# One kernel, one core: the last weight tiles of the final layer split earlier, and some subtractions placed elsewhere

## The chip, the core and the metric

The kernel runs on one core of a Trainium2 chip. TensorE (PE in the rows) does the matmuls, VectorE (DVE), ScalarE (ACT) and GpSimd (POOL) do the elementwise work, and SyncE (SP) issues nearly all transfers. Each engine works through its own list of instructions in order. The metric is the device time of one execution in microseconds (us); lower is better.

## The reference

Per batch and head a sigmoid attention, then a layer that takes the maximum of three products, then one more product:

```python
scores = scale * np.matmul(q, k.transpose(0, 1, 3, 2)) - np.log(S)
attn = 1.0 / (1.0 + np.exp(-scores))
out = np.matmul(attn, v)                       # 8 batches, 12 heads, 448 x 64
x = out.transpose(0, 2, 1, 3).reshape(B * S, H * D)   # 3584 x 768
h = np.maximum(np.maximum(x @ w1, x @ w2), x @ w3)
return h @ w_out
```

All inputs are float32. The kernel keeps the accuracy by splitting an operand into a rounded high part and the remainder (hi and lo), and by three matmuls for each product: lo times hi, hi times lo, hi times hi.

## The kernel before, in words

There are three parts. First comes the attention. Then the three products run as 12 visits (3 stages of 4 pairs of batches, numbered 0 to 11 in the code, so the sixth visit is visit 5). A visit is 3 x 7 = 21 products of 9 matmuls each; the seven products per weight are a Strassen-like scheme with sums of blocks. `order` holds the products as pairs (visit, place r of 21). Other engines prepare a visit's operands at given places: `his` and `los` split the next inputs, `ws` the next weights, and `decodes` names the places at which one tile of weights, which arrives as int64 words, is decoded (two ScalarE and four VectorE instructions, L220 to L231). Decoded tiles go back to DRAM (`w_dram`, weights of the third stage) or are added up on GpSimd (`l_sums`, L274, 15 sums for each group of three tiles of `wout`, stored to `wl_dram`).

The last layer is a scheme of 15 products (`STEPS`) for each of the 4 pairs of batches, so 60 steps; in the texts step g counts all 60. A step is 2 x 6 matmuls: two halves of the output (q), each into its own PSUM bank. Banks come in chains A, B and C: a step either starts a chain afresh or adds to it, and a result must have been read out (L928 on ScalarE, L932 on VectorE) before the chain is written again.

What a step needs:

- A weight tile pair whi, wlo. There are 20 tiles (j = 0 to 19) of three blocks; a step uses four blocks, and tiles 14 to 19 are used from step 10 on. `wl_load(j)` loads a tile, `wl_hi(j)` (L721, ScalarE) rounds it, `wl_lo(j)` (L725, VectorE) subtracts.
- An input pair xhi, xlo: a loaded block (`l_load`) or a difference of two (`l_sum`, L677, GpSimd), rounded by ScalarE (`l_hi`, L699) and subtracted by VectorE (`l_lo`, L709). The blocks and sums lie in buffers that are handed out from the list `slots` and come back when their last reader is done.
- For the steps that `room(v, s)` names, ScalarE also copies the input to PSUM (`ps_av`, L702), and VectorE subtracts from that copy instead of from the buffer in SBUF.

`plan` says what is done where: place 0 is the product 21 places ahead of the last layer (`BEFORE`), place 21 + g is step g. `l_plan(at)` runs the entries of a place ahead of that step's matmuls. The rounding for step g stands at step g - 3 and the subtraction at step g - 2.

Of the kernel before, what the change touches and what calls it, by code (L numbers as in the profile page):

```python
# [101 lines left out]
def attention_then_maxout(  # L102
# [54 lines left out]
    def w_tiles(q, name):  # L157
        hi = w_p.tile([P, HP], F32R, name=f"whi_{name}_{q}")
        lo = w_p.tile([P, HP], F32R, name=f"wlo_{name}_{q}")
        w_ops[q][name] = hi, lo  # L160
        return hi, lo
# [31 lines left out]
    def raw_tile(dec_p, name, words=HP):  # L193
        return dec_p.tile([P, words], I64, name=name, bufs=1)
# [457 lines left out]
    slots = ["xs_b11", "xs_t2", "xs_b12", "xs_b21", "xs_t1", "xs_t4", "xs_b22"]  # L652
# [3 lines left out]
    plan = {}  # L656

    def l_take_raw(key):

        name = slots.pop(-1 if key in ((0, "s8"), (0, "s16")) else 0)  # L660
        if name[:2] == "wr":
            t = raw_tile(dec_p, name, S).bitcast(F32).rearrange("p (a s) -> p a s", s=S)
        elif name[:2] == "xs":
            t = xs_p[name == "xs_t4"].tile([P, HALF, S], F32, name=name)
        else:
            t = xo_p[1].tile([P, HALF, S], F32R, name=name).bitcast(F32)
        l_raw[key] = t[:, :2], name

    def l_load(v, name):
        l_take_raw((v, name))  # L670
        j, th = divmod(int(name[1]), 2)
        pin(nc.sync.dma_start(out=l_raw[v, name][0], in_=h_dram[v][:, th, j]))

    def l_sum(v, name):
        l_take_raw((v, name))
        a, b = (l_raw[v, x][0] for x in X_SUMS[name])
        pin(nc.gpsimd.tensor_tensor(out=l_raw[v, name][0], in0=a, in1=b, op=ALU.subtract))  # L677


    ROOM = (4, 7, 9, 10, 11, 12, 14, 0, 1)  # L680

    def room(v, s):
        return s in (ROOM if v else (7, 9, 10, 14))

    def l_hi(v, s):
        g, x = v * len(STEPS) + s, l_raw[v, STEPS[s][1]][0]
        if g:
            name = SETS[(g - 1) % len(SETS)]
            to = xo_p[name not in FIRST]
            hi, lo = (  # L690
                to.tile([P, HALF, S], F32R, name=f"x{part}_{name}")[:, :2] for part in ("hi", "lo")
            )
        else:
            both = wl_p[0].tile([P, len(L_SUMS) * P], F32R, name="sums")
            hi, lo = (
                both[:, k * 2 * S : (k + 1) * 2 * S].rearrange("p (a s) -> p a s", a=2)
                for k in range(2)
            )
        pin(nc.scalar.copy(out=hi, in_=x))  # L699
        if room(v, s):  # L700
            px = ps_av.tile([P, 2, 512], F32, name="ps_av")
            pin(nc.scalar.copy(out=px[:, :, :S], in_=x))  # L702
            x = px[:, :, :S]
        l_ops[g], l_px[g] = (hi, lo), x
# [8 lines left out]
    def wl_load(j):  # L713
        q, k = divmod(j, len(PRODUCTS))
        wl_ops[j] = w_tiles(q, PRODUCTS[k][0])
        src = wl_dram[:].rearrange("p s b c -> p (s b c)")[:, j * HP : (j + 1) * HP]
        pin(nc.sync.dma_start(out=wl_ops[j][1].bitcast(F32), in_=src))

    def wl_hi(j):
        hi, lo = wl_ops[j]  # L720
        pin(nc.scalar.copy(out=hi, in_=lo.bitcast(F32)))  # L721

    def wl_lo(j):
        hi, lo = wl_ops[j]
        pin(nc.vector.tensor_tensor(  # L725
            out=lo, in0=lo.bitcast(F32), in1=hi.bitcast(F32), op=ALU.subtract
        ))

    events = []
    for v in pairs:  # L730
        for s, (_, x, *_) in enumerate(STEPS):
            events.append((v, s - 3, 1, l_hi, s, (x,)))
            events.append((v, s - 2, 0, l_lo, s, () if room(v, s) else (x,)))
        events += [(v, s, 2, l_sum, x, X_SUMS[x]) for s, x in X_AT.items()]
        events += [(v, s, 3, l_load, x, ()) for s, xs_ in LOADS.items() for x in xs_]
# [30 lines left out]
    for k, e in enumerate(events):  # L766
        plan.setdefault(place(*e), []).append(lambda k=k: l_event(k))
    WL_LOADS = (1, 2, 3, 4, 5, 7, 8, 8, 9, 10, 11, 12, 14, 15, 15, 16, 17, 18, 19, 20)
    WL_SPLITS = (4, 5, 6, 7, 8, 10, 11, 11, 12, 13, 14, 15, 17, 18, 28, 29, 30, 31, 32, 33)
    for j, (at, split_at) in enumerate(zip(WL_LOADS, WL_SPLITS)):  # L770
        plan.setdefault(at, []).append(lambda j=j: wl_load(j))
        plan.setdefault(split_at, []).append(lambda j=j: wl_hi(j))
        plan.setdefault(split_at + 1, []).insert(0, lambda j=j: wl_lo(j))

    def l_plan(at):
        for run in plan.get(at, ()):
            run()

    decodes = {n: (6, 8, 10) for n in (3, 4, 5, 6, 8, 9, 10)}
    decodes = {0: (10,), 1: (8,), 2: (8,), **decodes, 5: (6, 8, 10, 12)}  # L780
    decodes = [(n, r) for n in decodes for r in decodes[n]]
    todo = [(1, 2, 3)] + [(2, q, n) for q in range(3) for n in range(4)]
    todo += [(STAGES, u, n) for u in range(2) for n in range(2 * HALF)]
    background = decoding(dec_p, todo, 1, 3, c_p, S)
# [38 lines left out]
    for at, (n, r, old, q, k) in enumerate(order):  # L823
# [21 lines left out]
        if here in his:  # L845
            to, name = his.pop(here)
# [8 lines left out]
        if here in x_loads:  # L855
            to, name = x_loads.pop(here)
# [87 lines left out]
    for g in range(end + 1):  # L944
        v, s = divmod(g, len(STEPS))
# [53 lines left out]
```

## Time and profile before

| | us |
|---|---|
| median of 3 runs | 864.03 (863.51 to 865.03) |
| the profiled execution, its own time | 862.89 |
| its span, first to last instruction | 861.1 |
| PE busy in the span | 848.9 |
| DVE, ACT, POOL busy | 618.8, 508.5, 240.0 |
| mean granted TensorE clock | 0.993 of full speed |

The profile is that of one execution. PE's busy time counts overlapping matmuls once, and a stretch in which PE neither waits nor slows down reads as fully busy. The idle time in brackets behind a row is what the engine waited just before it, and for which instruction.

### The profile page before, as it was taken

How to read it: one execution, taken by the hardware profiler on the slowest of the kernel's cores; microseconds unless marked ns; L12 is line 12 of the kernel's file. 1: busy time of each engine (PE TensorE's matmuls, PEld its weight loads, DVE VectorE, ACT ScalarE, POOL GpSimd, SP SyncE). 2: the span in 40 equal slices, each digit the busy share in tenths (PEclk: the TensorE clock that was granted, in tenths of full speed). 3: DMA queues.
4: the chain of work that ended last, by engine and by line, in shares of the span. 5: the costliest groups of instructions: out<-in, count | busy, mean ns of one | idle time of the engine just before them, and what ended most of it. 6: DMA issues, size and time to landing. Idle time of an engine off the chain costs nothing. (4 is left out here: it accounts for less than half of the span.)

```text
span 861.1 us, 14454 instructions
## 1 busy us (share of the span) xinstructions
PE 848.9 (99%) x5410; PEld 700.2 (81%) x5410; DVE 618.8 (72%) x820; ACT 508.5 (59%) x715; POOL 240.0 (28%) x192
## 2 busy tenths in 40 slices
PE   9999999999999999999999999999999999899998
PEld 5555555555579999999998999999999898699997
DVE  5677668877786766766577674567667778997895
ACT  6888888888873442544444453445445447477774
POOL 0010020102007248112000322230302707668660
PEclk9999999999999999999999999999999999799999
DMA  8666777786675647346484822649462754245413
GB/s 290 210 211 229 250 249 234 256 302 226 207 248 219 222 174 256 133 132 244 144 281 146 290 77 69 208 143 326 132 231 68 247 178 132 99 154 197 148 68 129
DMA packets 79878, 166.95 MB, mean 194 GB/s; under 512 B 7616, under 2 KB 55744, under 8 KB 79808
## 3 DMA queue, kind: packets, MB, share of 16 engines
q1 hardware_dynamic: 79664, 165.92, 56.1%
q8 instruction: 42, 0.69, 0.3%
q14 instruction: 28, 0.23, 0.1%
q10 hardware_dynamic: 144, 0.11, 0.0%
HBM read 113.31 MB, written 52.69 MB: 193 GB/s over the span
## 5 line engine op out<-in xcount | busy, mean ns | idle before, releaser
L801 ACT COPY ps_y<-ps_y 128x448 f32<-128x448 f32 x72 | 37.3, 518 | 167.9 <-PE ps_y L598 144.2
L407 ACT ACTIVATE a<-ps_s,bias_s 128x896 f32<-128x896 f32 x121 | 114.6, 1017 | 11.0 <-PE ps_s L437 11.0
L598 PE MATMUL ps_y<-xhi_t,wlo_s 128*128 128x448 f32 x324 | 117.5, 363 | 0.0
L598 PE MATMUL ps_y<-xlo_t,whi_s 128*128 128x448 f32 x324 | 117.1, 361 | 0.0
L598 PE MATMUL ps_y<-xhi_t,whi_s 128*128 128x448 f32 x324 | 117.1, 361 | 0.0
L178 POOL TENSOR_TENSOR ws_s<-ws_a,ws_a 128x384 f32<-128x384 f32 x9 | 10.4, 1158 | 285.3 <-DMA ws_a<-w_dram 179.4
L598 PE MATMUL ps_y<-xhi_b,wlo_a 128*128 128x448 f32 x216 | 78.5, 363 | 0.0
L598 PE MATMUL ps_y<-xlo_b,whi_a 128*128 128x448 f32 x216 | 78.1, 362 | 0.0
L598 PE MATMUL ps_y<-xhi_b,whi_a 128*128 128x448 f32 x216 | 78.0, 361 | 0.0
L598 PEld LDWEIGHTS ps_y<-xhi_t,whi_s 128*128 128x128 f32 x324 | 60.7, 187 | 4.6
L598 PEld LDWEIGHTS ps_y<-xhi_t,wlo_s 128*128 128x128 f32 x324 | 60.8, 188 | 3.8
L598 PEld LDWEIGHTS ps_y<-xlo_t,whi_s 128*128 128x128 f32 x324 | 60.7, 187 | 3.8
L461 PE MATMUL ps_av<-a,v 64*64 64x448 f32 x576 | 62.6, 536 | 0.0
L356 DVE TENSOR_TENSOR xlo_t<-xs_t,xhi_t 128x1344 fp32r<-128x1344 f32 x30 | 47.5, 1586 | 17.2 <-ACT xhi_t L352 15.2
L461 PE MATMUL ps_s<-a,v 64*64 64x448 f32 x576 | 59.7, 544 | 0.0
L816 DVE TENSOR_TENSOR c<-ps_y,p 128x448 f32<-128x448 f32 x48 | 29.9, 622 | 38.0 <-PE ps_y L598 36.9
L419 DVE TENSOR_TENSOR lo<-qk,hi 128x896 fp32r<-128x896 f32 (+4 forms) x51 | 53.5, 1049 | 1.8
L356 DVE TENSOR_TENSOR xlo_b<-xs_b,xhi_b 128x1344 fp32r<-128x1344 f32 x30 | 49.4, 1646 | 0.0
L352 ACT CAST xhi_t<-xs_t 128x1344 fp32r<-128x1344 f32 x30 | 39.6, 1320 | 14.8 <-PE ps_y L598 13.5
L461 PEld LDWEIGHTS ps_av<-a,v 64*64 64x64 f32 x576 | 22.0, 133 | 32.1 <-issue 32.1
L437 PE MATMUL ps_s<-hi 64*128 64x448 f32 x240 | 46.8, 386 | 0.0
L230 DVE CUSTOM_DVE_ANT_0 wb<-wraw,wb 128x768 uint16<-128x768 uint16 x48 | 28.6, 597 | 22.3 <-ACT wraw L221 18.7
(216 smaller groups left out, 2214.1 us busy)
## 6 DMA issues: line engine op xcount, KB each, us to landing
qk<-qk SPq DMA_DIRECT2D x47, 448.0 KB, 4.7
xs_b<-x_dram SPq DMA_DIRECT2D x30, 672.0 KB, 6.2
wraw<-w SPq DMA_DIRECT2D x36, 384.0 KB, 5.0
xs_t<-t_dram SPq DMA_DIRECT2D x18, 672.0 KB, 6.5
v<-v SPq DMA_DIRECT2D x24, 448.0 KB, 5.6
h_dram<-m SPq DMA_DIRECT2D x48, 224.0 KB, 2.1
x_dram<-m SPq DMA_DIRECT2D x47, 224.0 KB, 2.9
t_dram<-xs_t SPq DMA_DIRECT2D x12, 672.0 KB, 3.1
```

What stands on the lines that cost most here:

```text
L178: pin(nc.gpsimd.tensor_tensor(out=r[name], in0=r[in0], in1=r[in1], op=op))
L230: pin(nc.vector.tensor_tensor(out=bits, in0=bits, in1=low, op=ALU.add))
L352: pin(copy(out=hi, in_=r[name]))
L356: pin(nc.vector.tensor_tensor(out=lo, in0=x, in1=hi.bitcast(F32), op=ALU.subtract))
L407: pin(nc.scalar.activation(out=a, in_=banks[:, :, :S], func=AF.Sigmoid, bias=bias_s, scale=scale))
L419: pin(nc.vector.tensor_tensor(out=lo[:, cols], in0=t[:, cols], in1=high.bitcast(F32), op=ALU.subtract))
L437: pin(nc.tensor.matmul(bank[e][:, :S], kt[r, S + c * P : S + (c + 1) * P], qt[r, :S], start=n == 0, stop=n == len(terms) - 1,))
L461: pin(nc.tensor.matmul(ps[e * D : (e + 1) * D, :S], vt[rows, (g * C + c) * 2 + e], chunks[c][rows, e], start=c == 0 and not (ahead and r = ...
L598: pin(nc.tensor.matmul(ps[:, :S], wt[:, k * P : (k + 1) * P], xt[:, k], start=first and n == 0, stop=n == len(terms) - 1, skip_group_check ...
L801: pin(nc.scalar.copy(out=bank(cycle, b)[:, :S], in_=y[:, :S]))
L816: pin(nc.vector.tensor_tensor(out=c, in0=y, in1=add, op=ALU.add))
```

## The change

Four edits. The six last weight tiles are rounded at places 19 to 24 and subtracted at places 20 to 25, where they stood at 28 to 33 and 29 to 34. For tiles 5 to 11 the subtraction stands one or two places later than before, which puts it behind evacuations of PSUM on VectorE. In the first pair of batches steps 11 and 12 get a copy in PSUM as well. The input `s9` of the first pair takes the buffer at the end of `slots`. And the fourth decoding of visit 5 is gone, with one at place 5 of visit 7 instead, so that every decoding between them is of the tile that was one earlier in turn.

```diff
-        name = slots.pop(-1 if key in ((0, "s8"), (0, "s16")) else 0)
+        name = slots.pop(-1 if key in ((0, "s9"), (0, "s8"), (0, "s16")) else 0)
...
     ROOM = (4, 7, 9, 10, 11, 12, 14, 0, 1)
 
     def room(v, s):
-        return s in (ROOM if v else (7, 9, 10, 14))
+        return s in ROOM and (v or s > 4)
...
     WL_LOADS = (1, 2, 3, 4, 5, 7, 8, 8, 9, 10, 11, 12, 14, 15, 15, 16, 17, 18, 19, 20)
-    WL_SPLITS = (4, 5, 6, 7, 8, 10, 11, 11, 12, 13, 14, 15, 17, 18, 28, 29, 30, 31, 32, 33)
-    for j, (at, split_at) in enumerate(zip(WL_LOADS, WL_SPLITS)):
-        plan.setdefault(at, []).append(lambda j=j: wl_load(j))
-        plan.setdefault(split_at, []).append(lambda j=j: wl_hi(j))
-        plan.setdefault(split_at + 1, []).insert(0, lambda j=j: wl_lo(j))
+    WL_HIS = (4, 5, 6, 7, 8, 10, 11, 11, 12, 13, 14, 15, 17, 18, 19, 21, 21, 22, 23, 24)
+    WL_LOS = (5, 6, 7, 8, 9, 13, 13, 14, 14, 15, 15, 16, 18, 19, 20, 22, 22, 23, 24, 25)
+    for j, (load_at, hi_at, lo_at) in enumerate(zip(WL_LOADS, WL_HIS, WL_LOS)):
+        plan.setdefault(load_at, []).append(lambda j=j: wl_load(j))
+        plan.setdefault(hi_at, []).append(lambda j=j: wl_hi(j))
+        plan.setdefault(lo_at, []).insert(0, lambda j=j: wl_lo(j))
...
-    decodes = {0: (10,), 1: (8,), 2: (8,), **decodes, 5: (6, 8, 10, 12)}
-    decodes = [(n, r) for n in decodes for r in decodes[n]]
+    decodes = {0: (10,), 1: (8,), 2: (8,), **decodes, 7: (5,)}
+    decodes = [(n, r) for n in sorted(decodes) for r in decodes[n]]
```

The first place is VectorE from the end of visit 11 to step 6 of the last layer. `m12` is the last evacuation of visit 11, `p3` and `wd0` are the two of step 1, the L709 rows are the subtractions for steps 4 to 8. Before:

```order
L725 TENSOR_TENSOR wlo_s4_1_7270<-wlo_s4_1_7270,whi_s4_1_7269 128x384
L709 TENSOR_TENSOR xlo_b21_7329<-wraw2_7144,xhi_b21_7328 128x896
L813 TENSOR_TENSOR m12_7120<-ps_y2_7265,m12_7120 128x448
L932 TENSOR_TENSOR p3_7374<-ps_y1_7385,p3_7374 128x448
L932 TENSOR_TENSOR wd0_7383<-ps_y1_7393,wd0_7383 128x448
L709 TENSOR_TENSOR xlo_b11_7402<-xs_b12_7037,xhi_b11_7401 128x896
L709 TENSOR_TENSOR xlo_t2_7426<-xs_t4_7217,xhi_t2_7425 128x896
L932 TENSOR_TENSOR m12_7435<-ps_y2_7406,m12_7435 128x448
L932 TENSOR_TENSOR m21_7444<-ps_y3_7415,m21_7444 128x448
L709 TENSOR_TENSOR xlo_t3_7448<-ps_av_7450,xhi_t3_7447 128x896
L709 TENSOR_TENSOR xlo_b21_7472<-xs_t2_7179,xhi_b21_7471 128x896
```

In the change (lines from L770 on are one higher, so L932 is L933):

```order
L725 TENSOR_TENSOR wlo_s4_1_7270<-wlo_s4_1_7270,whi_s4_1_7269 128x384
L709 TENSOR_TENSOR xlo_b21_7329<-wraw2_7144,xhi_b21_7328 128x896
L814 TENSOR_TENSOR m12_7120<-ps_y2_7264,m12_7120 128x448
L725 TENSOR_TENSOR wlo_a11_2_7273<-wlo_a11_2_7273,whi_a11_2_7272 128x384
L725 TENSOR_TENSOR wlo_s3_2_7311<-wlo_s3_2_7311,whi_s3_2_7310 128x384
L725 TENSOR_TENSOR wlo_s2_2_7292<-wlo_s2_2_7292,whi_s2_2_7291 128x384
L933 TENSOR_TENSOR p3_7378<-ps_y1_7392,p3_7378 128x448
L933 TENSOR_TENSOR wd0_7387<-ps_y1_7400,wd0_7387 128x448
L725 TENSOR_TENSOR wlo_a12_2_7333<-wlo_a12_2_7333,whi_a12_2_7332 128x384
L725 TENSOR_TENSOR wlo_s1_2_7352<-wlo_s1_2_7352,whi_s1_2_7351 128x384
L709 TENSOR_TENSOR xlo_b11_7410<-xs_b12_7037,xhi_b11_7409 128x896
L725 TENSOR_TENSOR wlo_a22_2_7367<-wlo_a22_2_7367,whi_a22_2_7366 128x384
```

Six L725 rows, tiles 14 to 19, have come in: three ahead of step 1's evacuations, two behind them, one behind the subtraction for step 5.

The second place is VectorE at steps 8 to 12, from the subtraction for step 10 on. Before:

```order
L725 TENSOR_TENSOR wlo_a11_2_7273<-wlo_a11_2_7273,whi_a11_2_7272 128x384
L709 TENSOR_TENSOR xlo_t2_7518<-ps_av_7520,xhi_t2_7517 128x896
L932 TENSOR_TENSOR p3_7374<-p3_7374,ps_y1_7428 128x448
L932 TENSOR_TENSOR wd0_7383<-wd0_7383,ps_y1_7437 128x448
L725 TENSOR_TENSOR wlo_s2_2_7292<-wlo_s2_2_7292,whi_s2_2_7291 128x384
L709 TENSOR_TENSOR xlo_t3_7544<-xs_t2_7496,xhi_t3_7543 128x896
L932 TENSOR_TENSOR m11_7413<-m11_7413,ps_y0_7367 128x448
L932 TENSOR_TENSOR m22_7422<-m22_7422,ps_y0_7376 128x448
L725 TENSOR_TENSOR wlo_s3_2_7311<-wlo_s3_2_7311,whi_s3_2_7310 128x384
L709 TENSOR_TENSOR xlo_b21_7566<-xhi_t1_7522,xhi_b21_7565 128x896
L725 TENSOR_TENSOR wlo_a12_2_7333<-wlo_a12_2_7333,whi_a12_2_7332 128x384
L709 TENSOR_TENSOR xlo_b11_7590<-wraw2_7546,xhi_b11_7589 128x896
```

In the change:

```order
L709 TENSOR_TENSOR xlo_t2_7530<-ps_av_7532,xhi_t2_7529 128x896
L933 TENSOR_TENSOR p3_7378<-p3_7378,ps_y1_7439 128x448
L933 TENSOR_TENSOR wd0_7387<-wd0_7387,ps_y1_7448 128x448
L709 TENSOR_TENSOR xlo_t3_7554<-ps_av_7556,xhi_t3_7553 128x896
L933 TENSOR_TENSOR m11_7422<-m11_7422,ps_y0_7371 128x448
L933 TENSOR_TENSOR m22_7431<-m22_7431,ps_y0_7380 128x448
L709 TENSOR_TENSOR xlo_b21_7576<-ps_av_7578,xhi_b21_7575 128x896
L709 TENSOR_TENSOR xlo_b11_7600<-xlo_t1_7558,xhi_b11_7599 128x896
```

The L725 rows are gone, and the subtractions for steps 11 (`xlo_t3`) and 12 (`xlo_b21`) read `ps_av` instead of a buffer; the one for step 13 (`xlo_b11`) still reads a buffer.

The third place is VectorE in visit 5, after the third decoding there. Before:

```order
L813 TENSOR_TENSOR m11_4998<-ps_y0_5024,m11_4998 128x448
L222 TENSOR_SCALAR wb_5116<-wraw0_5047 128x384
L226 SCALAR_TENSOR_TENSOR wb_5116<-wraw0_5047,wb_5116 128x384
L230 ISA wb_5116<-wraw0_5047,wb_5116 128x768
L231 SCALAR_TENSOR_TENSOR wb_5116<-c_5115,wb_5116 128x384
L816 TENSOR_TENSOR c_5133<-ps_y2_5078,p3_5101 128x448
L817 TENSOR_TENSOR m22_5011<-c_5133,m22_5011 128x448
```

In the change:

```order
L814 TENSOR_TENSOR m11_4998<-ps_y0_5024,m11_4998 128x448
L817 TENSOR_TENSOR c_5122<-ps_y2_5078,p3_5101 128x448
L818 TENSOR_TENSOR m22_5011<-c_5122,m22_5011 128x448
L817 TENSOR_TENSOR c_5149<-ps_y1_5034,p3_5101 128x448
L818 TENSOR_TENSOR m21_5045<-c_5149,m21_5045 128x448
```

The fourth decoding stood between `m11` and the two evacuations, `c` with `m22` and `c` with `m21`; now nothing stands there.

## Rows read from the trace of the kernel before

**Rows 1.** Stretches of the last layer: length, busy (count) of PE, PEld, DVE, ACT, POOL; PEclk.
```profile
701.60:727.80 26.20, 26.20 (x133) 24.56 (x132) 19.05 (x23) 16.90 (x25) 12.84 (x6) 1.00 0.49 162
727.80:746.70 18.90, 13.33 (x42) 9.44 (x40) 18.54 (x15) 5.75 (x8) 18.45 (x8) 0.73 0.27 95
746.70:856.90 110.20, 110.08 (x549) 102.84 (x549) 92.57 (x102) 79.07 (x106) 59.94 (x24) 1.00 0.41 142
```

**Rows 2.** Waits of PE over the whole span: us in total, times, longest.
```profile
PE ps_y L889 <- DVE xlo_b L709: 2.9, 2, 1.9
PE ps_y L889 <- DVE m L932: 1.7, 1, 1.7
PE ps_y L598 <- DVE c L816: 1.5, 2, 0.8
PE ps_y L889 <- DVE wlo_a L725: 0.9, 2, 0.8
```

**Rows 3.** PE's timeline in the last layer: start us, us, instruction, [idle before <- releaser].
```profile
701.66 0.36 PE L889 MATMUL ps_y<-sums,wlo_a 128*128 128x448 f32 x1
...
727.86 0.37 PE L889 MATMUL ps_y<-xhi_t,whi_a 128*128 128x448 f32 x1
...
745.47 0.58 PE L889 MATMUL ps_y<-xhi_t,whi_s 128*128 128x448 f32 x1
746.80 0.47 PE L889 MATMUL ps_y<-xhi_t,wlo_a 128*128 128x448 f32 x1 [0.76 <-DVE wlo_a L725]
```

**Rows 4.** Groups of DVE instructions from 721 to 747: count, busy us, mean ns.
```profile
L725 DVE TENSOR_TENSOR wlo_a<-wlo_a,whi_a 128x384 fp32r<-128x384 f32 x3 | 6.5, 2170 | 0.5 <-ACT whi_a L721 0.4
L725 DVE TENSOR_TENSOR wlo_s<-wlo_s,whi_s 128x384 fp32r<-128x384 f32 x3 | 3.4, 1123 | 0.0
L709 DVE TENSOR_TENSOR xlo_t<-ps_av,xhi_t 128x896 fp32r<-128x896 f32 x3 | 3.2, 1077 | 0.0
...
L709 DVE TENSOR_TENSOR xlo_t<-xs_t,xhi_t 128x896 fp32r<-128x896 f32 x1 | 3.0, 3017 | 0.0
```

**Rows 5.** DVE's timeline in the last layer's first steps, and at 746.67.
```profile
702.13 0.55 DVE L725 TENSOR_TENSOR wlo_s<-wlo_s,whi_s 128x384 fp32r<-128x384 f32 x1
...
705.53 0.62 DVE L932 TENSOR_TENSOR p<-ps_y,p 128x448 f32<-128x448 f32 x1 [1.31 <-PE ps_y L889]
706.73 0.62 DVE L932 TENSOR_TENSOR wd<-ps_y,wd 128x448 f32<-128x448 f32 x1 [0.58 <-PE ps_y L889]
...
710.47 1.09 DVE L709 TENSOR_TENSOR xlo_t<-xs_t,xhi_t 128x896 fp32r<-128x896 f32 x1 [1.74 <-ACT xhi_t L699]
...
746.67 1.08 DVE L709 TENSOR_TENSOR xlo_t<-ps_av,xhi_t 128x896 fp32r<-128x896 f32 x1
```

**Rows 6.** POOL's timeline: its first sum in the last layer, and a later one.
```profile
713.78 2.14 POOL L677 TENSOR_TENSOR xs_b<-xs_b,xs_t 128x896 f32<-128x896 f32 x1 [23.99 <-ACT ps_av L702]
...
728.24 2.97 POOL L677 TENSOR_TENSOR xs_t<-wraw,xlo_t 128x896 f32<-128x896 f32 x1
```

**Rows 7.** ACT's timeline: a copy to PSUM.
```profile
743.30 0.91 ACT L702 COPY ps_av<-xlo_t 128x896 f32<-128x896 f32 x1 [9.64 <-DVE xlo_t L709]
```

**Rows 8.** Timelines of DVE and PE in visit 5, and of PE in visit 11.
```profile
458.36 0.36 DVE L222 TENSOR_SCALAR wb<-wraw 128x384 uint32<-128x384 uint32 x1 [1.45 <-issue]
...
460.52 0.62 DVE L816 TENSOR_TENSOR c<-ps_y,p 128x448 f32<-128x448 f32 x1
...
460.00 0.36 PE L598 MATMUL ps_y<-xhi_t,whi_a 128*128 128x448 f32 x1
461.19 0.47 PE L598 MATMUL ps_y<-xhi_b,wlo_s 128*128 128x448 f32 x1 [0.83 <-DVE c L816]
...
688.95 0.47 PE L598 MATMUL ps_y<-xhi_b,wlo_s 128*128 128x448 f32 x1 [0.68 <-DVE c L816]
```

**Rows 9.** Timelines of DVE and POOL in visit 7.
```profile
520.96 0.62 DVE L811 TENSOR_TENSOR m<-ps_y,p 128x448 f32<-128x448 f32 x1 [2.84 <-issue]
...
532.76 1.01 POOL L178 TENSOR_TENSOR ws_s<-ws_a,ws_a 128x384 f32<-128x384 f32 x1 [31.85 <-DMA ws_a<-w_dram]
```

## The prediction

> **What bounds the kernel now.** PE does. I read its waits first [rows 2]: over the whole span only some 7 us, all on VectorE, most of them in the last layer (L889). Then the stretches of that layer [rows 1]: PE is busy throughout in the first and the third, and in the second, 727.8 to 746.7, for 13.33 of 18.90 us, at a granted clock of 0.73. VectorE is busy there for 18.54 of 18.90 us and GpSimd for 18.45, ScalarE for 5.75. So in this one stretch VectorE sets the pace; everywhere else PE does, and an edit elsewhere can win nearly nothing.
>
> What the stretch costs comes from PE's timeline [rows 3]. The layer starts at 701.66; the matmul at 727.86 closes step 10 (11 x 12 = 132 matmuls), so the undisturbed pitch is 26.20 / 131 = 0.200 us and a step takes 2.40. At 746.80, 549 of the 720 matmuls are left [rows 1], so this is number 172, 40 behind the one at 727.86. They took 18.94 us and want 8.00: **10.94 us are lost**. 5.6 of it is idle time (18.90 - 13.33); the rest is pace: a matmul is 0.58 long at 745.47 against 0.37 at 727.86, and the mean clock of 0.73 lies between the two levels (1.2 and 2.4 GHz), so PE ran at the lower one for part of the stretch, after it had stood still several times. Behind 746.80 nothing is lost: 549 matmuls fill 110 us at 0.200.
>
> **Why VectorE is late there.** A subtraction reads two operands. Those that read PSUM took 1.08 us beside a working GpSimd, one of the same size that reads a buffer 3.02 [rows 4]; with GpSimd at rest it took 1.09 (710.47 in [rows 5]). GpSimd's sums stretch too, from 2.14 to 2.97 [rows 6]. The two engines take turns: 3.02 - 1.08 = 1.94, nearly one sum. The weight subtractions suffer likewise: 2.17 and 1.12 us on average [rows 4] against 0.55 at 702.13 [rows 5].
>
> **The last six weight tiles, and steps 11 and 12.** At 746.67 the subtraction for step 15 starts and ends at 747.75 [rows 5]. Undisturbed, step 15 would start at 701.66 + 15 x 2.40 = 737.66: VectorE is 10.09 us late, about PE's loss. Gone from the queue ahead of it are six weight subtractions, 3 x 2.17 + 3 x 1.12 = 9.87, and twice 3.02 - 1.08 = 3.88: 13.75 us. So it would end 3.7 us ahead of need. Followed row by row in the new order it is similar: VectorE then waits mostly for evacuations to be ready (1.47 and 2.67 us behind a step's start, from 705.53 and 706.73 with step 1 at 704.06) and for ScalarE's copies. ScalarE gets two more copies of 0.91 [rows 7]. A copy must wait until the subtraction ahead has left ps_av; its 9.64 us of waiting there is VectorE's lateness handed on and goes with it. Copy plus subtraction are 2.0 us of a 2.40 us step, so four such steps in a row (9 to 12) hold the pace. The term is the whole 10.94, clock included, since PE doesn't stop. Bounds: 0 if another wait takes its place, 10.94 at most.
>
> **Where the six tiles go.** ScalarE was busy for 16.90 of the first stretch's 26.20 us [rows 1], so six roundings, each shorter than its 0.91 us copy [rows 7], find room. The tiles' loads keep their places in SP's list. VectorE has, from 704 to 711, idle pieces of 1.31, 0.58 and 1.74 us [rows 5], 3.6 in all, for six subtractions of 0.55 = 3.3. What is queued behind them are the evacuations p3 and wd0, and for these PE waits: step 3 starts both B banks afresh at 701.66 + 7.20 = 708.86. GpSimd was at rest before 713.78, for 23.99 us [rows 6]. Here the `s9` edit matters: its sum was GpSimd's last before that rest, over by 689.8 (713.78 - 23.99); now its buffer is xlo_b22, which visit 11 reads to its last product, so the sum runs from about 701.7 to 703.9, beside VectorE. One block of about 2 us: the subtraction at 702.13 ends at 704.4, the one for step 4 at 705.4, m12 at 705.9, three weight tiles at 707.3, p3 at 707.9, wd0 at 708.4. That is 0.9 us ahead of step 3 and 1.6 ahead of its second half (710.06). Then two tiles to 709.4 and the subtraction for step 5 to 710.4 (needed at 713.66). The next sum still waits for the same copy at step 4. I take nothing; bounds 0 and, with a second block, 1.2 us.
>
> **The decoding.** The fourth one in visit 5 ran from 458.36 ahead of c, which started at 460.52; PE's matmul at 461.19 waited for it [rows 8]. The matmul ahead, at 460.00, wants its successor at 460.20: 0.99 us lost. In the new order c can start when its product ends, two products (3.6 us) before 460.20, so **0.99 us** is won. In visit 7 the decoding comes at place 5, ahead of an evacuation at 520.96 with 2.84 us of idle before it [rows 9]; a decoding takes VectorE 2.2 us (458.36 to 460.52), more where ScalarE's half comes late: the evacuation may be up to 1 us late, and PE writes that bank again two products, 3.6 us, behind. The 15 sums of the first three `wout` tiles move from visit 6 to visit 7, where GpSimd rests for 31.85 us up to 532.76 [rows 9]. The transfers move along: the last third-stage tile is stored 15 products later and read near the end of visit 7, and on SP the stores of the sums fall among weight loads that GpSimd waits for with time to spare. Cost 0; if the cover were gone, one c late as in visit 5, 0.99.
>
> **The subtractions behind evacuations.** At 688.95 PE stands idle for 0.68 us for the same kind of c [rows 8], about 0.85 lost (0.99 went with 0.83 of idle above). The rows that VectorE works through ahead of that c are the same and in the same order in the change; only what follows it moves. So I keep that loss: 0, with a bound of 0.85 won.
>
> **The sum.** 862.89 - 10.94 - 0.99 = 850.96 for an execution like the profiled one (span 849.2). The median of the runs is 1.14 above that execution: **852.1 us**.
>
> **The rivals.**
>
> *The wait comes back in the second pair.* GpSimd keeps its pace on the wall clock while PE is 11 us earlier, so VectorE loses the lead that PE's stop gave it. A pair asks VectorE for 18 evacuations of 0.62 (11.2), nine subtractions from PSUM (9.7) and six from buffers, 1.08 to 3.02 each: 27.4 to 39.0 us against 36.0. In the third stretch it was busy for 92.57 of 110.20 with no wait of PE [rows 1], so GpSimd doesn't hit all six. If it does, 3.0 us a pair are lost, 9.0 over three pairs, and 861.1 comes out; half of that is likelier, 856.6. Following the queue with every clash taken, the slimmest leads I find are 0.6 to 1.2 us, at steps 20 to 24. The Trainium skill speaks for this rival ("SBUF — State Buffer", section "SBUF: two separate sides"): the engine that starts first holds a shared port pair for its whole instruction and the other is blocked entirely. By that rule the six would wait a full sum, 1.08 + 2.14 = 3.22 each, 40.2 us a pair, 12.6 us over three, 864.7 in the end; the trace agrees with the taking of turns (3.02), and against the sum that sums must be there to clash with: 11 of 2.14 fill 23.5 of 36 us.
>
> *The edit doesn't remove what PE waits for.* Only 0.9 us of the last layer's waits name a weight tile (L725); the others name inputs and an evacuation [rows 2]. If only these went, with the clock 0.9 x 1.95 = 1.8, and 0.99 in visit 5, it is 861.2. Against it: VectorE works in order, and the weight tiles stand ahead of those others.
>
> *Slower: the six tiles stop PE early.* If GpSimd worked from 702 to 712, six subtractions at 2.17 instead of 0.55 (9.7) and two inputs at 3.02 (3.9) against 3.6 of idle make VectorE 10.0 us late at step 6; with the clock (10.94 lost for 5.6 idle, 1.95 to 1) PE loses 19.5, and 871.6 comes out. It decides from 6.1 us of lateness (6.1 x 1.95 = 11.9), that is from five sums there (5 x 1.94 - 3.6 = 6.1); I find one.
>
> *The loss at 688.95 goes too*, if the phase of GpSimd beside it shifts: 851.2.
>
> **How the numbers follow.** Forecast, with 688.95 kept: 0.60; with it gone: 0.19; second pair: 0.12; weight tiles not the cause: 0.05; early stop: 0.04. A measurement of this kernel tells about 0.2% (1.7 us; its runs spread over 1.5) from no change. Faster: all but the early stop and a little of the second pair: 0.95; same 0.02; slower 0.03. The range: 851.2 less 0.6 of spread below; above, the second pair's milder half: 850.6 to 856.0.
>
> **What would show it.** Right: PE's waits in the last layer gone, a clock of 1.00 there, step 15's subtraction ahead of its step, 0.55 us for the six tiles, c of visit 5 some 3 us earlier. Wrong: a wait of PE on p or wd at step 3, a wait on L709 or L933 at steps 20 to 24, or the lower clock anywhere behind 702.

## The result and the profile after

The changed kernel takes **850.2 us** (median of 4 runs, 849.70 to 851.24), the kernel before beside it on the same chip 864.3 (4 runs, 863.51 to 865.03): a ratio of 0.9839 (0.9822 to 0.9856), 14.1 us faster. The forecast was 852.1 with a range of 850.6 to 856.0. The direction and the places were right; the time lies 1.9 us under the forecast and 0.4 under the range.

The profiled execution took 849.70 us, with a span of 847.9 and a mean granted clock of 1.000 (before: 862.89, 861.1, 0.993). What is left of PE's waits over the whole span of the changed kernel (us in total, times, longest), the answer to [rows 2]:

```profile
PE ps_s L508 <- PEq L988: 0.8, 1, 0.8
PE ps_y L598 <- DVE c L817: 0.2, 1, 0.2
```

Every wait of the last layer is gone, and one of the two on c; the 0.8 on PE's own sequencer (PEq) in the attention stood there before as well. (The matmul line L889 is L890 now, L932 is L933, L816 is L817.) Next the stretches of the last layer, cut as long as in [rows 1] where that goes; the columns are the same: length, busy time (count) of PE, PEld, DVE, ACT, POOL, and PEclk (the last two, the DMA's, are not used).

```profile
699.50:725.70 26.20, 26.20 (x132) 24.56 (x132) 23.11 (x31) 18.16 (x26) 15.37 (x8) 1.00 0.52 174
725.70:744.60 18.90, 18.90 (x96) 17.71 (x96) 14.47 (x17) 14.39 (x20) 18.82 (x8) 1.00 0.61 226
744.60:843.90 99.30, 99.10 (x496) 92.56 (x494) 83.25 (x92) 69.92 (x93) 58.21 (x24) 1.00 0.37 130
```

In the second stretch PE is now busy for all of 18.90 us at a clock of 1.00, and runs 96 matmuls where 42 were recorded. VectorE has 4.4 us to spare there, against 0.4 before. GpSimd is as busy as ever (18.82): what bounded the stretch was VectorE's queue, which GpSimd lengthens, and not GpSimd itself. In the first stretch VectorE went from 19.05 to 23.11 us: that is where the six tiles and one blocked subtraction now stand. PE's first and last matmul of the layer:

```profile
699.53 0.36 PE L890 MATMUL ps_y<-sums,wlo_a 128*128 128x448 f32 x1
...
843.33 0.37 PE L890 MATMUL ps_y<-xhi_t,whi_a 128*128 128x448 f32 x1
```

843.33 - 699.53 = 143.80 = 719 x 0.200: the layer runs from end to end at its pitch. Before, the first started at 701.66 [rows 3] and the last one here:

```profile
856.52 0.37 PE L889 MATMUL ps_y<-xhi_t,whi_a 128*128 128x448 f32 x1
```

That is 154.86, so 11.06 us were lost there.

VectorE's timeline of the changed kernel in the layer, the answer to [rows 4, 5]:

```profile
700.00 2.48 DVE L725 TENSOR_TENSOR wlo_s<-wlo_s,whi_s 128x384 fp32r<-128x384 f32 x1
702.41 1.08 DVE L709 TENSOR_TENSOR xlo_b<-wraw,xhi_b 128x896 fp32r<-128x896 f32 x1
...
703.95 0.54 DVE L725 TENSOR_TENSOR wlo_a<-wlo_a,whi_a 128x384 fp32r<-128x384 f32 x1
704.41 1.01 DVE L725 TENSOR_TENSOR wlo_s<-wlo_s,whi_s 128x384 fp32r<-128x384 f32 x2
705.35 0.61 DVE L933 TENSOR_TENSOR p<-ps_y,p 128x448 f32<-128x448 f32 x1
...
731.47 1.08 DVE L709 TENSOR_TENSOR xlo_t<-ps_av,xhi_t 128x896 fp32r<-128x896 f32 x1
...
744.34 2.60 DVE L709 TENSOR_TENSOR xlo_b<-wraw,xhi_b 128x896 fp32r<-128x896 f32 x1 [0.34 <-ACT xhi_b L699]
...
749.33 2.65 DVE L709 TENSOR_TENSOR xlo_t<-xs_t,xhi_t 128x896 fp32r<-128x896 f32 x1
```

The first moved tiles take 0.54 us each (703.95, and 1.01 for the next two; the other three 0.54 to 0.56) where [rows 4] has 1.12 and 2.17. p for step 3 ends at 705.96; step 3 starts at 699.53 + 7.20 = 706.73, so 0.77 us are left. The subtraction for step 15 ends at 732.55, 3.0 ahead of its step (735.53), where it was 10.09 late. In the second pair the ones for steps 21 and 23 still meet GpSimd's sums (2.60 and 2.65 us), but end at 746.94 and 751.98 with their steps at 749.93 and 754.73: 2.8 to 3.0 ahead. GpSimd's sums in the layer, the answer to [rows 6]:

```profile
699.58 2.49 POOL L677 TENSOR_TENSOR xlo_b<-xs_b,xs_b 128x896 f32<-128x896 f32 x1 [14.29 <-PE ps_y L598]
711.66 2.15 POOL L677 TENSOR_TENSOR xlo_b<-xs_b,xs_t 128x896 f32<-128x896 f32 x1 [9.59 <-ACT ps_av L702]
```

The first is `s9`, moved as forecast to the layer's start. The subtraction at 700.00 started inside it and ended at 702.48, 0.41 behind the sum's end at 702.07. The Trainium skill ("SBUF — State Buffer", section "SBUF: two separate sides") says that of a GpSimd operation that reads SBUF and a VectorE one with two SBUF inputs the first holds a shared port pair to its end and the other is blocked; this row agrees (2.48 us, where the same subtraction takes 0.55 in `all_but_s9`, below).

Visits 5, 7 and 11, the answer to [rows 8, 9], first on VectorE (the decoding of visit 7 ends at 520.05), then on PE:

```profile
457.27 0.61 DVE L817 TENSOR_TENSOR c<-ps_y,p 128x448 f32<-128x448 f32 x1
...
519.49 0.56 DVE L231 SCALAR_TENSOR_TENSOR wd<-c,wb 128x384 f32<-128x384 f32 x1
519.97 0.62 DVE L812 TENSOR_TENSOR m<-ps_y,p 128x448 f32<-128x448 f32 x1
522.85 0.62 DVE L812 TENSOR_TENSOR m<-ps_y,p 128x448 f32<-128x448 f32 x1 [2.27 <-PE ps_y L598]
```

```profile
459.65 0.36 PE L598 MATMUL ps_y<-xhi_b,wlo_s 128*128 128x448 f32 x1
...
686.25 0.36 PE L598 MATMUL ps_y<-xhi_t,whi_a 128*128 128x448 f32 x1
686.82 0.47 PE L598 MATMUL ps_y<-xhi_b,wlo_s 128*128 128x448 f32 x1 [0.21 <-DVE c L817]
```

In visit 5 c starts 3.25 us earlier than before (457.27 for 460.52; 0.55 of it is the whole program, below) and PE's matmul follows at the pitch. In visit 7 the evacuation at 519.97 starts right behind the decoding, about half a microsecond late (before it started at 520.96, and PE is 0.55 + 0.99 = 1.54 us earlier now, so it was wanted at 519.4), and PE doesn't notice. In visit 11 the wait that I kept is 0.21 us instead of 0.68; the loss there is 0.57 - 0.20 = 0.37 instead of 0.85.

**The account of the two profiled executions.** The spans differ by 13.2 us: 11.06 in the layer, 0.99 in visit 5, 0.48 in visit 11, 0.55 ahead of the visits, 0.1 not placed. The 0.55 lies ahead of everything that the change touches, at the first matmul of the visits, before and after:

```profile
245.89 0.48 PE L598 MATMUL ps_y<-xhi_b,wlo_a 128*128 128x448 f32 x1
```

```profile
245.34 0.48 PE L598 MATMUL ps_y<-xhi_b,wlo_a 128*128 128x448 f32 x1
```

### The profile page after: what moved, and what is told of

Read it like the earlier page. It is cut to its first block, busy times and chain, and to the rows that moved or that the text cites. A ratio compares the mean times of both kernels' runs of the same rounds, so it can differ in the third digit from the quotient of the medians.

```text
span 847.9 us, 14455 instructions
## 1 busy us (share of the span) xinstructions
PE 842.7 (99%) x5410; PEld 698.2 (82%) x5410; DVE 606.2 (71%) x820; ACT 511.0 (60%) x717; POOL 240.9 (28%) x192
## 4 chain that ended last, share of the span: by engine, by line
PE 98%; DVE 1%; DMA 0%; issue 0%; ACT 0%
PE ps_y L598 52%; PE ps_y L890 17%; PE ps_s L437 9%; PE ps_s L461 7%; PE ps_av L461 6%; PE ps_s L472 2%; PE ps_s L450 2%; PE ps_av L437 2%; DMA wlo_a<-wl_dram 0%; DVE sums L709 0%; PE ps_s L508 0%; DVE wlo_s L725 0%; DVE wlo_a L725 0%; PE ps_av L450 0%; PE ps_av L472 0%; DVE c L817 0%
## 5 line engine op out<-in xcount | busy, mean ns | idle before, releaser
L817 DVE TENSOR_TENSOR c<-ps_y,p 128x448 f32<-128x448 f32 x48 | 29.9, 623 | 41.3 <-PE ps_y L598 40.5
```

What stands on the lines that cost most here:

```text
L817: pin(nc.vector.tensor_tensor(out=c, in0=y, in1=add, op=ALU.add))
```

## The experiments

Twelve sets of runs, in three groups of four; each group shared a chip with runs of the kernel before, and ratios are to those. The first group is the next section (median of the kernel before 863.4 us); `after_again`, `all_but_room`, `five_sums` and `also_a12_s1` are the second (865.25), the other four the third (863.22). A difference between kernels of two groups is one between chips as well. **Theory**, as the runs left it: the six weight tiles ahead of step 15 made VectorE late, and their move alone gives back the layer's whole loss; the decoding gives 0.99 more; copies, `s9` and the reordered subtractions add nothing to that. (The expectation of `only_tiles` still counted the copies as needed.) **Rivals:** the copies for steps 11 and 12 carry part of the gain (by the forecast's ledger 3.88 of 13.75); or the weight tiles are not the cause.

### Each part alone, and all but the tiles

`only_tiles` is the kernel before with the table's last six entries changed:

```
-    WL_SPLITS = (..., 17, 18, 28, 29, 30, 31, 32, 33)
+    WL_HIS = (..., 17, 18, 19, 21, 21, 22, 23, 24)
+    WL_LOS = (..., 18, 19, 20, 22, 22, 23, 24, 25)
```

> The kernel before with only the last six weight tiles moved to places 19 to 25. Queue theory (VectorE's work beside GpSimd is the cause, the six tiles are 9.9 of the 13.8 us taken away): step 12's and 13's inputs still take 3 us each and come 1 to 2 us late, so most of the 10.9 us goes: 854.5 to 856.5 us. Rival (the inputs that VectorE reads from buffers are the cause, the tiles only stand in the queue): 861 or more.

Measured 851.38 us (850.86 to 851.67), ratio 0.9855 (0.9838 to 0.9872): 12.0 us of the 14.1, without copies, `s9` or decoding. Its waits of PE, all in the visits, its chain in the layer (start, us, count), and its VectorE at steps 11 to 13:

```profile
PE ps_y L598 <- DVE c L817: 1.6, 3, 0.9
```

```profile
701.32 144.02 PE ps_y L890 x720
```

```profile
723.49 2.37 DVE L709 TENSOR_TENSOR xlo_t<-xs_t,xhi_t 128x896 fp32r<-128x896 f32 x1
...
726.85 1.96 DVE L709 TENSOR_TENSOR xlo_b<-xhi_t,xhi_b 128x896 fp32r<-128x896 f32 x1
728.74 3.02 DVE L709 TENSOR_TENSOR xlo_b<-wraw,xhi_b 128x896 fp32r<-128x896 f32 x1
```

The chain is one piece of 720 matmuls. Steps 11 and 12 read buffers and take 2.37 and 1.96 us, yet step 13's subtraction ends at 731.76, 0.76 ahead of 701.32 + 13 x 2.40 = 732.52. The expectation was 3 to 5 us too slow: it counted the copies as part of what removes the wait.

`all_but_tiles` is the change with those six entries as before:

```
-    WL_HIS = (..., 17, 18, 19, 21, 21, 22, 23, 24)
-    WL_LOS = (..., 18, 19, 20, 22, 22, 23, 24, 25)
+    WL_HIS = (..., 17, 18, 28, 29, 30, 31, 32, 33)
+    WL_LOS = (..., 18, 19, 29, 30, 31, 32, 33, 34)
```

> The change without the move of the six tiles. Queue theory: 3.9 of 10.1 us of lateness gone, 6.2 left, so some 6 us slower than the change: 855 to 859 us, with PE waiting from step 11 or 12 on. Rival (inputs from buffers): within 1 us of the change, 850 to 851.5.

Measured 859.44 (858.23 to 860.92), ratio 0.995 (0.9933 to 0.9967). The waits of the layer are back:

```profile
PE ps_y L890 <- DVE m L933: 1.8, 1, 1.8
PE ps_y L890 <- DVE xlo_b L709: 1.4, 1, 1.4
PE ps_y L890 <- DVE wlo_s L725: 1.1, 1, 1.1
PE ps_y L890 <- DVE wlo_a L725: 0.9, 1, 0.9
```

With the tiles in the old place everything else gives 4.0 us; the tiles give 12.0 alone and 9.2 on top of the rest (859.44 to 850.2). So the terms overlap: copies and tiles free the same VectorE time, and whichever comes second finds less to win (4.0 is also more than the 1.7 and 0.8 that copies and decoding give alone, below, within the spread of these kernels).

`only_room` is the kernel before with the copies for steps 11 and 12:

```
-        return s in (ROOM if v else (7, 9, 10, 14))
+        return s in ROOM and (v or s > 4)
```

> The kernel before with only the copies to PSUM for steps 11 and 12. Queue theory: about 4 us won, 858.5 to 862 us. Rival (inputs from buffers): nearly all of the last layer's loss won, 853 to 855.

Measured 861.74 (860.15 to 864.5), ratio 0.9981 (0.9968 to 0.9993): 1.7 us. Three of its waits:

```profile
PE ps_y L890 <- DVE xlo_b L709: 2.1, 2, 1.6
PE ps_y L890 <- DVE wlo_a L725: 2.0, 1, 2.0
...
PE ps_y L890 <- DVE m L933: 1.8, 1, 1.8
```

Two copies take 3.88 us off VectorE by the ledger and only 1.7 off the time. The six tiles still follow and PE waits for those; in the profiled execution they take 11.57 us from 721 to 745 where they took 9.87 before, so GpSimd's sums now hold up weight tiles instead.

`only_decode` is the kernel before with the decoding moved:

```
-    decodes = {0: (10,), 1: (8,), 2: (8,), **decodes, 5: (6, 8, 10, 12)}
+    decodes = {0: (10,), 1: (8,), 2: (8,), **decodes, 7: (5,)}
```

> The kernel before with only the decoding moved from visit 5 to visit 7. My term: 0.99 us won, 863.3 us, with no wait of PE on c in visit 5 and the last layer as before. Rival (the wait moves to visit 6 or 7): 864.3, and a wait on c of about 0.8 us in another visit.

Measured 862.62 (858.5 to 863.56), ratio 0.9983 (0.9969 to 0.9998): 0.8 us, with no wait of PE left in visit 5; its only wait on c is the one in visit 11 (0.66), so it did not move to visit 6 or 7. The term was 0.99. "The last layer as before" holds for its waits but not for its length, as the part on the sum shows.

### The change again, and without one part

`after_again` is the changed kernel, for the spread.

> The changed kernel once more, on the chip of the next three. All theories: 849.5 to 851 us, and no wait of PE in the last layer.

Measured 850.21 (849.83 to 850.36), ratio 0.9826 (0.9802 to 0.9849). The wait on c in visit 11 was 0.5 us here and 0.2 in the first profile: one program, two sizes.

`all_but_room` takes the copies back (the edit of `only_room` reversed).

> The change without the copies to PSUM for steps 11 and 12. With the tiles moved alone PE already had no wait in the last layer, so the queue theory now says: the same as the change, 849.5 to 851 us, inputs of steps 11 and 12 at 2 to 3 us each. My prediction counted these copies with 3.9 of the 13.8 us; if they were needed, 851.5 to 853.

Measured 849.95 (849.78 to 850.39), ratio 0.9825 (0.9802 to 0.9849), no wait in the layer, with the inputs of steps 11 and 12 at 2.40 and 1.97 us as expected. The copies are worth nothing once the tiles are moved.

`all_but_decode` takes the decoding back to visit 5.

> The change with its decoding left at the sixth visit (visit 5). The sum by terms: 0.99 us above the change, so some 851.0 to 851.4, with one wait of TensorE on c of 0.8 to 0.95 us at 460 to 462 and none in the last layer. Rival: the loss of visit 5 was made up elsewhere in the change, and the time stays at 850.2 (within 0.3).

Measured 851.82 (849.98 to 851.99), ratio 0.9868 (0.9848 to 0.9887). The four runs are 849.98, 851.73, 851.92 and 851.99, and the profiled one was the fastest, with a small wait in visit 5:

```profile
459.92 0.47 PE L598 MATMUL ps_y<-xhi_b,wlo_s 128*128 128x448 f32 x1 [0.42 <-DVE c L817]
```

By the median the decoding is worth 1.6 us against the change and 1.8 to 2.0 against the other three kernels on this chip, which differ from the change by nothing measurable; `only_tiles` against the change says 1.2, `only_decode` 0.8. The same place cost between 0.42 and 1.35 us of idle time in four profiled kernels (this one 0.42, before 0.83, `only_tiles` 0.93, `only_room` 1.35), so 0.99 was one draw of a cost that varies.

`all_but_s9` gives the sum its old buffer:

```
-        name = slots.pop(-1 if key in ((0, "s9"), (0, "s8"), (0, "s16")) else 0)
+        name = slots.pop(-1 if key in ((0, "s8"), (0, "s16")) else 0)
```

> The change with the buffer of the sum s9 taken as before, so that GpSimd makes this sum before the last layer begins. The step of the prediction that costs the sum at nothing says: time as of the change, 850.2 within 0.4, no wait of TensorE in the last layer, the 2.5 us subtraction at 700 back at 0.55 us, and the evacuation p at step 3 some 2 us more ahead of need than the 0.77 of the change. Rival: the late sum also holds back GpSimd's next ones and with them VectorE's later clashes; then this kernel is 0.5 to 1 us off in one direction and its waits name the place.

Measured 849.79 (849.66 to 850.64), ratio 0.9845 (0.9828 to 0.9862). VectorE's first weight tile in the layer, and GpSimd's first sum there:

```profile
700.93 0.55 DVE L725 TENSOR_TENSOR wlo_s<-wlo_s,whi_s 128x384 fp32r<-128x384 f32 x1
```

```profile
712.58 2.13 POOL L677 TENSOR_TENSOR xs_b<-xs_b,xs_t 128x896 f32<-128x896 f32 x1 [23.98 <-ACT ps_av L702]
```

The block of 2.48 us is gone and GpSimd rests again for 24 us, and the time is the same: one blocked subtraction there costs nothing.

`all_but_order` puts the reordered weight subtractions back behind their roundings. (By the lists only those of tiles 5 to 9 had moved; tiles 10 and 11 have the same place in both.)

```
-    WL_LOS = (5, 6, 7, 8, 9, 13, 13, 14, 14, 15, 15, 16, 18, ...)
+    WL_LOS = (5, 6, 7, 8, 9, 11, 12, 12, 13, 14, 15, 16, 18, ...)
```

> The change with the weight subtractions of tiles 5 to 11 at the places that they had before, one behind each rounding. The prediction costs this reordering at nothing: 850.2 within 0.4, at most one wait on c of 0.3 to 0.7 us at 686 to 689. Rival: the reordering is what took away part of the wait at 688; then this kernel has a wait on c of over 0.7 us there and takes 850.6 to 851.2.

Measured 850.03 (849.67 to 850.41), ratio 0.9846 (0.983 to 0.9863), the wait on c 0.6 us. No difference that can be told.

### Doubling a suspected cost, and going further

`five_sums` makes the sum `s9` five times over on GpSimd, to test where the early stop begins:

```
+        for _ in range(5 if (v, name) == (0, "s9") else 1):
             pin(nc.gpsimd.tensor_tensor(out=l_raw[v, name][0], ...))
```

> The change with the sum s9 of the first pair done five times over on GpSimd (same operands, same result, so only time is added) while VectorE subtracts the moved tiles. Rival of the prediction (early stop): each sum blocks one of VectorE's subtractions by 1.9 us, p and wd of step 1 come some 6 us late, PE stops at step 3 and its clock falls: 857 to 862 us. If the engines don't block each other there: 849.5 to 851.

Measured 858.61 (858.16 to 859.64), ratio 0.9925 (0.9905 to 0.9945), 8.4 us above `after_again`. Its waits of PE in the layer, then GpSimd and VectorE (the lines are one number higher):

```profile
PE ps_y L891 <- DVE p L934: 4.4, 1, 4.4
PE ps_y L891 <- DVE m L815: 1.6, 1, 1.6
```

```profile
700.21 12.53 POOL L678 TENSOR_TENSOR xlo_b<-xs_b,xs_b 128x896 f32<-128x896 f32 x5 [14.29 <-PE ps_y L598]
```

```profile
700.64 2.48 DVE L726 TENSOR_TENSOR wlo_s<-wlo_s,whi_s 128x384 fp32r<-128x384 f32 x1
703.05 3.02 DVE L710 TENSOR_TENSOR xlo_b<-wraw,xhi_b 128x896 fp32r<-128x896 f32 x1
705.98 0.61 DVE L815 TENSOR_TENSOR m<-ps_y,m 128x448 f32<-128x448 f32 x1
706.52 1.92 DVE L726 TENSOR_TENSOR wlo_a<-wlo_a,whi_a 128x384 fp32r<-128x384 f32 x1
708.37 4.79 DVE L726 TENSOR_TENSOR wlo_s<-wlo_s,whi_s 128x384 fp32r<-128x384 f32 x2
713.08 0.61 DVE L934 TENSOR_TENSOR p<-ps_y,p 128x448 f32<-128x448 f32 x1
```

Five sums block exactly five subtractions: these take 12.21 us instead of 3.18 (0.55 as in `all_but_s9`; 1.08, 0.54 and 1.01 as in the change), 1.8 a clash where the forecast's rival put 1.94. m, which reads PSUM, is late but not stretched (0.61). p comes at 713.08, 12.9 us behind the layer's first matmul (700.17) where it was 5.8 in the change, and PE stands for 4.36 and 1.61 us: 5.97 of idle time, near the 6.1 of lateness that the rival worked out. So the mechanism of the slower rival is real, and the change escapes it because only one sum stands there. The clock falls as well: granted 0.50 in the 4 us from 713.70. The price was set too high: the layer's matmuls run from 700.17 to 853.26, 153.09, which is 9.29 lost. 6.38 of it is how late p lets PE go on (at 713.75, wanted at 700.17 + 7.20 = 707.37), and 2.91 follows behind it, where the clock is low.

`also_a12_s1` is the change with the subtractions of weight tiles 3 and 4 moved away from visit 11's c:

```
-    WL_LOS = (5, 6, 7, 8, 9, 13, 13, ...)
+    WL_LOS = (5, 6, 7, 13, 14, 13, 13, ...)
```

> The change with the subtractions of weight tiles 3 and 4 also moved behind the evacuations (places 13 and 14 instead of 8 and 9). If the wait on c in visit 11 comes from these two subtractions, which take 2.5 us each beside GpSimd's sums: that wait is gone, 0.4 us won, 849.3 to 850.3 us. If it comes from the rows ahead of them: as the change, with the wait.

Measured 849.79 (849.74 to 850.45), ratio 0.9823 (0.98 to 0.9847). PE waits for VectorE nowhere any more, and VectorE waits for PE ahead of the first c there, which starts at 683.00 where the change has 686.16:

```profile
683.00 0.62 DVE L817 TENSOR_TENSOR c<-ps_y,p 128x448 f32<-128x448 f32 x1 [1.25 <-PE ps_y L598]
```

So those two subtractions were what made c late; by the medians that is 0.4 us, within the spread.

`tiles_decode` keeps only what the runs showed to matter (tiles, decoding, and the subtractions of `also_a12_s1` with the reordering), without copies and with the old `s9`.

> What the earlier runs leave as needed: the six tiles at steps 0 to 4, the decoding in the eighth visit and the reordering, with the subtractions of weight tiles 3 and 4 put later too; no copies for steps 11 and 12, and the sum s9 with its old buffer. If these carry the whole gain: 849.5 to 850.3 and no wait of TensorE on VectorE at all. Rival: the copies and the old sum are each covered only while the other is there; then waits return at steps 11 to 15 and the time is 851 or more.

Measured 849.95 (849.62 to 850.42), ratio 0.9846 (0.9829 to 0.9862), no wait of PE on VectorE. Neither of these two can be told from the change; they are simpler or cleaner, not measurably faster.

## Why the prediction was right in its mechanism and wrong in its number

**What bounds the kernel; why VectorE is late.** Right, except that idle time and pace are not two parts of the cost that add up (see the sum). The layer's loss was VectorE's lateness, handed on; with it gone PE runs through. The term of 10.94 measured 11.06 in the profiled executions.

**The last six weight tiles, and steps 11 and 12.** Right in sum, wrong in the split. The forecast needed 13.75 us off VectorE's queue against 10.09 of lateness and added 3.88 for the copies to 9.87 for the tiles. `only_tiles` shows that the tiles do it alone, and `all_but_room` that the copies add nothing. A ledger of busy time doesn't say which part is needed where slack behind it absorbs the rest: steps 11 and 12 cost 2.37 and 1.96 us there, not twice 3.02, and the lead of 0.76 at step 13 was enough.

**Where the six tiles go.** Right: one block (2.48 us), p 0.77 us ahead of step 3 (forecast 0.9), nothing lost; `all_but_s9` shows the block to cost nothing. `five_sums` shows the edge of it, with the idle time near the forecast's arithmetic.

**The decoding.** The place was right and visit 7 cost nothing. The size was one execution's: between 0.8 and 2.0 us by comparisons of medians.

**The subtractions behind evacuations.** "So I keep that loss: 0" was mis-sized. 0.48 of the 0.85 was won in the first profile. The rows ahead of c are the same, but the wait is not fixed by them: 0.2 and 0.5 us in two executions of the changed kernel, too short to be listed in `all_but_decode`, 0.3 to 0.7 in the others that keep these rows. This loss should have been forecast as a spread, 0 to 0.85.

**The sum.** The step that put the time outside the range is the last one: "The median of the runs is 1.14 above that execution". It adds that distance to the changed kernel as if every kernel carried it. Every run is its span and nearly a constant: in 41 runs of the kernel before, time less span is 1.73 to 1.86. So the 1.14 was a longer span and no overhead. The traces show where such a length comes from. `only_decode` differs from the kernel before only in the visits, and in the layer VectorE works through the same rows in the same order. What follows PE's last wait in the layer, first before, then in `only_decode`, and the first 4 us of it with the columns of [rows 1]:

```profile
746.80 110.10 PE ps_y L889 x549
745.32 112.25 PE ps_y L890 x549
```

```profile
746.80:750.80 4.00, 4.00 (x20) 3.75 (x21) 4.00 (x5) 3.02 (x5) 0.00 (x0) 1.00 0.30 115
745.30:749.30 4.00, 3.98 (x11) 3.54 (x12) 4.00 (x5) 2.42 (x4) 0.00 (x0) 0.50 0.30 115
```

Up to that wait both lose the same, 10.94 and 11.00 us (their layers start at 701.66 and 700.12), though PE idles 5.7 us in the one and 7.8 in the other: VectorE sets the pace there, and a slower PE only waits less. Behind it the kernel before loses 0.12 and `only_decode` 2.28, because its clock is still at the lower level (0.50). So the layer of the same rows lost 11.06 in one execution and 13.28 in another, and the forecast's 10.94 came from the lower of the two. The distance to the median belongs, as far as these two traces tell, to the stall that the change removes, and should not have been added.

The spreads fit that. Spans of the kernel before go from 858.6 to 866.5, with clocks of 0.991 to 0.998; in the changed kernel and the five others with neither the layer's wait nor visit 5's (29 runs), times lie between 849.62 and 851.24, with clocks of 0.998 to 1.000. Of the kernels that still wait in the layer, `only_room` spreads over 4.35 us, `only_decode` 5.1 and `all_but_tiles` 2.7, but `five_sums` over 1.5 only (12, 12, 6 and 6 runs). How the executions without a trace divide is not shown.

The changed kernel's median is 0.5 above its profiled execution, so 0.64 of the 1.9 is this step; the other 1.26 is the difference between 850.96 and 849.70: 0.48 in visit 11, 0.55 ahead of the visits, 0.12 in the layer, 0.11 not placed. The 0.55 is no effect of the change, so that part of the miss is chance. The range inherited the 1.14 at its low end; from 850.96 - 0.85 - 0.6 = 849.5 upward it would have held 850.2.

**The rivals.** The second pair didn't come: leads of 2.8 to 3.0 us where the worst case left 0.6 to 1.2, since not every subtraction meets a sum. That the tiles were not the cause is refuted by `only_tiles`; the waits that name a weight tile (1.1 us with the 0.2 on wlo_s, which the forecast's 0.9 left out) say little of what made the queue late. The early stop didn't come, and `five_sums` shows what it would have taken. Its price, lateness times 1.95, was wrong in kind: 1.95 is loss over PE's idle time, while the loss before was about VectorE's lateness itself (11.06 for 10.09) and in `five_sums` 9.29 for 6.38. "The loss at 688.95 goes too" came by half, by chance between executions as much as by the change.

## What to carry to other kernels

When one in-order engine sets the pace for a short stretch, look for work in its queue there whose inputs were ready long before, and move it to where that engine idles: here six subtractions moved to idle places gave 12 of the 14 us, and three other edits of the same change added nothing measurable to them. Parts that free the same engine's time don't add; price each alone and on top of the others. Don't carry the distance between a profiled execution and the median over to a kernel whose stall is removed: here the stall brought most of the variation, and both went together. Read what a stall costs from when the work behind it resumes, not from idle time times a rate. A small wait that hangs on the phase of another engine is a range and not a number.

## What the runs showed that was not expected

- PE's idle time is no measure of what the layer lost: 11.06 for 5.7 idle before, 13.28 for 7.8 in `only_decode`, 9.29 for 5.97 in `five_sums`, 7.9 for 5.23 in `all_but_tiles` (851.86 - 700.16 = 151.70, less 143.80). While PE waited for VectorE anyway, the lower clock cost nothing; behind the last wait it cost 0.1, 2.3, 2.9 and 0.1 us.
- GpSimd and VectorE alternate instruction by instruction when both have work on buffers: five sums, five blocked subtractions, 1.8 us each, while a subtraction from PSUM beside them keeps its 1.08 us and an evacuation its 0.61.
- A block of 2 us on VectorE at the start of the layer was free, and four more made the kernel 8.4 us slower: the lead of p over step 3 (0.77 us) is what was left of the slack.
